# Rewriting a four-layer hedgehog and softmax attention block: token-major residual, visits of query to key chunks, projections between attention steps

## Chip, cores, metric

The kernel runs on one core of one Trainium2 chip. The metric is the device time of one execution in microseconds (us); lower is better. A single core has no second die to compare with, so runs are called fast when they lie within 1.5% of the fastest of the same kernel; all runs of changed kernels below are fast, except one single run whose state is unknown (e14_part1). Engines are named as in the profile: PE is TensorE (matmul), PEld its weight loads, DVE VectorE, ACT ScalarE, POOL GpSimd, SP SyncE, which here only issues DMAs (SPq).

## The reference, cut

```python
S, D, H = 2048, 1024, 32; Dh = 32                  # bf16 everywhere
def A(x, wqkv, w_phi, wo):                         # hedgehog linear attention
    q, k, v = heads(x @ wqkv)
    pq, pk = q @ w_phi, k @ w_phi                  # per head, 32 x 32
    phi_q = concat(softmax(pq), softmax(-pq)); phi_k = the same of pk
    kv, z = phi_k.T @ v, sum(phi_k)                # over all 2048 tokens
    return (phi_q @ kv) / (phi_q @ z + 1e-6) -> merge heads -> @ wo
def B(x, wqkv, wo):                                # plain softmax attention
    q, k, v = heads(x @ wqkv)
    return softmax(q @ k.T * Dh**-0.5) @ v -> merge heads -> @ wo
x = x + A(ln(x)); x = x + B(ln(x)); x = x + A(ln(x)); x = x + B(ln(x))
```

Every A layer needs a sum over all tokens (kv, z) before its query part can start. Every B layer has 32 x 2048 x 2048 exponentials.

## The kernel before

It runs one stage after the other. The residual is kept transposed (features on partitions). A B layer projects everything, then attends, then projects out:

```python
iters = [(g, qc, kc) for g in range(G) for qc in range(NQ) for kc in range(NT)]
...
for ii, (g, qc, kc) in enumerate(iters):
    ...
    for pr in range(2):                             # two heads each
        nc.scalar.activation(out=e[:], in_=s_cur[pr][:], func=ACT.Exp)   # 128 x 1024
    ...
    emit_scores(g2, qc2, kc2, s_next)               # 4 row-tiled matmuls, K = 32
    for j in range(4):                              # 4 column-tiled: values
        nc.tensor.matmul(out=num_ps[hsl, :], lhsT=v_aug[:, kc, g, ...], rhs=e_tiles[pr][...], ...)
    for j in range(4):                              # 4 column-tiled: denominators
        nc.tensor.matmul(out=den_ps[hsl, :], lhsT=ones_bf[:, 0:DH], rhs=e_tiles[pr][...], ...)
    if kc == NT - 1:
        nc.vector.reciprocal(out=rden[:], in_=den_ps[:])       # 128 x 512
        nc.vector.tensor_tensor(out=oT[:, g, q_sl], in0=num_ps[:], in1=rden[:], op=ALU.mult)
```

An A layer computes the key projection twice, once for exp(+pk) and once for exp(-pk) (`for b in range(2): ... emit_pk(fc, t)`), and layer norm sums over features with matmuls against ones.

The softmax here doesn't subtract the row's maximum and nothing guards it: scores larger than these inputs give would overflow.

## Time and profile before

3484.5 us (median of 2 runs; 3484.05 to 3484.96).

| stage | us | what is busy |
|---|---|---|
| A layer and B projections, first time | 0 to 750 | PE and DVE; ACT 242 us |
| attention | 750 to 1687.5 | ACT all the time |
| the same again | 1687.5 to 2440 | PE and DVE; ACT 244 us |
| attention | 2440 to 3377 | ACT all the time |
| last output projection, store | 3377 to 3483.5 | PE, then DVE |

The first lines of the page of the kernel before: busy time, share of the span and count by engine, then busy tenths in 40 slices, with the granted TensorE clock in tenths of full speed.

```profile
span 3483.5 us, 44252 instructions
PE 3190.9 (92%) x18316; PEld 1118.3 (32%) x18432; DVE 1359.2 (39%) x2009; ACT 2360.9 (68%) x2688; POOL 0.7 (0%) x6
...
PE   2898679999999999999979976899999999999998
...
ACT  0125861039999999999312298100999999999970
...
PEclk9999989999999999999999988999999999999997
```

PE at 92% suggests a PE-bound kernel, but PE busy time is no proof of that: the Trainium skill ("Trainium Kernel Development and Optimization", Performance Expectations) warns that matmul busy time is a bad measure of how near a kernel is to its limit, because matmuls are pipelined. This trace agrees: in attention PE counts as busy for 936 of 937.5 us, and yet the scores that it makes wait for ACT, as the lines below show. Two windows of the kernel before, columns being the stretch, its length, then busy time (count) of PE, PEld, DVE, ACT, POOL, granted clock, DMA share and GB/s:

```profile
750.00:1687.50 937.50, 936.35 (x6134) 271.05 (x6132) 125.53 (x62) 937.38 (x1023) 0.00 (x0) 1.00 0.00 1
2440.00:3377.00 937.00, 936.68 (x6132) 271.12 (x6132) 125.53 (x62) 937.00 (x1024) 0.00 (x0) 1.00 0.00 1
```

The timeline of ACT in the kernel before, at the start of attention and 150 us later (start, duration, what):

```profile
750.12 1.02 ACT L295 ACTIVATE E_5251<-sps_5243 128x1024 bf16<-128x1024 f32 x1 [70.11 <-PE sps_5244 L274]
751.05 1.02 ACT L295 ACTIVATE E_5253<-sps_5244 128x1024 bf16<-128x1024 f32 x1
...
900.19 1.29 ACT L295 ACTIVATE E_6752<-spsn_6738 128x1024 bf16<-128x1024 f32 x1
901.11 1.29 ACT L295 ACTIVATE E_6754<-spsn_6739 128x1024 bf16<-128x1024 f32 x1
```

One exponential starts every 0.915 us while each takes 1.02 us, later 1.29 us: each is already waiting in ACT when the one before is still running. ACT sets the pace of attention, 1024 x 0.915 = 937 us per layer. In the other 1610 us ACT is busy for 486 us. That is the room that the change aims at.

### The profile page before, as it was taken

To read this page: it belongs to the slowest core of one execution; us is meant where nothing else is said; L and a number is where in the kernel's file an instruction comes from. 1 tells how busy PE (TensorE), PEld (TensorE's weight loads), DVE (VectorE), ACT (ScalarE), POOL (GpSimd) and SP (SyncE) were. 2 spreads that over 40 slices of the span, in tenths; PEclk is the share of its full clock that TensorE was granted. 3 is DMA by queue.
4 is the path that set the end of the run, shared out by engine and by line. 5 is a ranking of instruction groups with operands and counts; after the bars stand their busy time and mean duration, and the time that the engine had idled before them with its cause. 6 is when DMAs were issued, how large, how long until landed. Compare 5 with 4: busy or idle time off the path is not lost.

```text
span 3483.5 us, 44252 instructions
## 1 busy us (share of the span) xinstructions
PE 3190.9 (92%) x18316; PEld 1118.3 (32%) x18432; DVE 1359.2 (39%) x2009; ACT 2360.9 (68%) x2688; POOL 0.7 (0%) x6
## 2 busy tenths in 40 slices
PE   2898679999999999999979976899999999999998
PEld 1343224432222222222334422344222222222223
DVE  2978876621111111111288888566011111111114
ACT  0125861039999999999312298100999999999970
POOL 0000000000000000000000000000000000000000
PEclk9999989999999999999999988999999999999997
DMA  6000001320000000000310000043000000000001
GB/s 132 15 1 1 1 25 61 128 78 1 1 1 1 1 1 1 1 1 1 74 49 1 1 1 0 25 145 121 1 1 1 1 1 1 1 1 1 1 25 49
DMA packets 112170, 82.67 MB, mean 24 GB/s; under 512 B 54624, under 2 KB 103776, under 8 KB 111968
## 3 DMA queue, kind: packets, MB, share of 16 engines
q1 hardware_dynamic: 111968, 79.84, 7.9%
q8 instruction: 144, 2.36, 0.3%
q14 instruction: 58, 0.48, 0.0%
HBM read 63.05 MB, written 4.19 MB: 19 GB/s over the span
## 4 chain that ended last, share of the span: by engine, by line
PE 75%; ACT 11%; DVE 10%; SPq 2%; issue 1%; DMA 1%; ACTq 0%; DVEq 0%
PE num_ps L307 19%; PE den_ps L319 13%; PE ps L167 7%; PE ps L222 6%; PE ps L245 3%; PE pkps L422 3%; ACT L548 2%; ACT L546 2%; DVE tmp L131 2%; ACT ebt L509 2%; DVE phik L449 1%; DVE xnT L134 1%; DVE ssum L445 1%; ACT e L441 1%; PE ps L142 1%
## 5 line engine op out<-in xcount | busy, mean ns | idle before, releaser
L330 DVE RECIPROCAL rden<-den_ps 128x512 f32<-128x512 f32 x64 | 214.9, 3358 | 1626.9 <-PE den_ps L319 1626.9
L274 PEld LDWEIGHTS <-kT 32*128 32x128 bf16 x4096 | 311.7, 91 | 872.8 <-issue 872.8
L307 PEld LDWEIGHTS <-v_aug 128*32 128x32 bf16 x4096 | 197.1, 93 | 465.6 <-issue 465.6
L222 PE MATMUL ps<-xnc,wslab 128*128 128x512 bf16 x1004 | 230.8, 386 | 15.2 <-DVE xnc L134 13.4
L167 PE MATMUL ps<-oT,wo_t 128*128 128x512 bf16 x1000 | 226.4, 386 | 16.2 <-DMA wo_t<-in_B_wo_dram 14.6
L422 PE MATMUL pkps<-W_pk,xnT 128*128 128x512 bf16 x994 | 239.2, 379 | 1.4
L441 ACT ACTIVATE e<-pkps 128x512 bf16<-128x512 f32 x128 | 76.2, 597 | 225.8 <-PE pkps L422 197.9
L117 ACT ACT_TABLE_LOAD x16 | 20.5, 1283 | 298.8 <-DVE t_386 L114 94.4
L319 PEld LDWEIGHTS <-ones_bf 128*32 128x32 bf16 x4096 | 208.8, 95 | 0.0
L491 PE MATMUL pqps<-xnT,W_pq 128*128 128x512 bf16 x496 | 160.7, 440 | 1.5 <-issue 0.7
L167 PEld LDWEIGHTS <-wo_t 128*128 128x128 bf16 x1024 | 101.7, 99 | 149.8 <-issue 33.9
L222 PEld LDWEIGHTS <-wslab 128*128 128x128 bf16 x1024 | 101.4, 99 | 142.8 <-issue 27.6
L142 PE MATMUL ps<-wv,xnT 128*128 128x512 bf16 x502 | 117.0, 380 | 21.6 <-DVE xnT L134 20.2
L174 DVE TENSOR_TENSOR xT<-xT,ps 128x512 bf16<-128x512 bf16 x128 | 87.4, 687 | 123.6 <-PE ps L167 121.7
L422 PEld LDWEIGHTS <-xnT 128*128 128x128 bf16 x1024 | 95.2, 98 | 91.6
L245 PE MATMUL ps<-wslab,xnc 128*128 128x512 bf16 x504 | 111.4, 379 | 0.4
L445 DVE TENSOR_REDUCE ssum<-e 128x16 f32<-128x512 bf16 x128 | 87.6, 685 | 39.6 <-ACT e L441 38.7
L449 DVE TENSOR_TENSOR phik<-e,rs 128x512 bf16<-128x512 bf16 x128 | 88.0, 691 | 11.8
L491 PEld LDWEIGHTS <-W_pq 128*128 128x128 bf16 x512 | 55.9, 110 | 92.0 <-issue 52.5
L546 ACT ACT_TABLE_LOAD x64 | 82.1, 1283 | 1.1
L548 ACT ACT_TABLE_LOAD x64 | 82.1, 1283 | 1.1
L509 ACT ACTIVATE ebt<-pqps 128x512 bf16<-128x512 f32 x128 | 74.5, 598 | 11.8 <-PE pqps L491 5.8
(9623 smaller groups left out, 7096.0 us busy)
## 6 DMA issues: line engine op xcount, KB each, us to landing
wslab<-in_B_wqkv_dram SPq DMA_DIRECT2D x48, 1024.0 KB, 5.0
wo_t<-in_A_wo_dram SPq DMA_DIRECT2D x2, 2048.0 KB, 9.7
wv<-in_A_wqkv_dram SPq DMA_DIRECT2D x2, 2048.0 KB, 7.9
wo_t<-in_B_wo_dram SPq DMA_DIRECT2D x2, 2048.0 KB, 8.8
out_dram<-tr SPq DMA_DIRECT2D x16, 256.0 KB, 2.0
phi<-in_A_w_phi_dram SPq DMA_DIRECT2D x64, 2.0 KB, 1.6
wqT<-in_A_wqkv_dram SPq DMA_TRANSPOSE x16, 4.2
wkT<-in_A_wqkv_dram SPq DMA_TRANSPOSE x16, 4.2
```

The source lines that it names most:

```text
L142: nc.tensor.matmul(ps[:], lhsT=xn_lhsT_fn(po), rhs=wv[:, po, fc * C512:(fc + 1) * C512], start=(po == 0), stop=(po == PO - 1),)
L167: nc.tensor.matmul(ps[:], lhsT=wo_t[:, po, ft * P:(ft + 1) * P], rhs=oT[:, po, cs], start=(po == 0), stop=(po == PO - 1),)
L222: nc.tensor.matmul(ps[:], lhsT=wt[:, po, gi * P:(gi + 1) * P], rhs=xnc[:, po, :], start=(po == 0), stop=(po == PO - 1),)
L245: nc.tensor.matmul(ps[:], lhsT=xnc[:, po, st * P:(st + 1) * P], rhs=wt[:, po, :], start=(po == 0), stop=(po == PO - 1),)
L274: nc.tensor.matmul(out=s_tiles[pr][:, jj * C512:(jj + 1) * C512], lhsT=kT[prt, g, k_sl], rhs=qT[prt, g, q_sl], start=True, stop=True, tile ...
L307: nc.tensor.matmul(out=num_ps[hsl, :], lhsT=v_aug[:, kc, g, j * DH:(j + 1) * DH], rhs=e_tiles[pr][:, jj * C512:(jj + 1) * C512], start=(kc ...
L319: nc.tensor.matmul(out=den_ps[hsl, :], lhsT=ones_bf[:, 0:DH], rhs=e_tiles[pr][:, jj * C512:(jj + 1) * C512], start=(kc == 0), stop=(kc == ...
L330: nc.vector.reciprocal(out=rden[:], in_=den_ps[:])
L422: nc.tensor.matmul(ps[:], lhsT=xnT[:, po, t * P:(t + 1) * P], rhs=W_pk[:, po, fc * C512:(fc + 1) * C512], start=(po == 0), stop=(po == PO ...
L491: nc.tensor.matmul(ps[:], lhsT=W_pq[:, po, g * P:(g + 1) * P], rhs=xnT[:, po, cs], start=(po == 0), stop=(po == PO - 1),)
L546: nc.scalar.activation(out=t3_list[gg][:], in_=t3_list[gg][:], func=ACT.Ln)
L548: nc.scalar.activation(out=t3_list[gg][:], in_=t3_list[gg][:], func=ACT.Exp, scale=-1.0)
```

## The change

The intent: keep ACT at its exponentials while PE does projections between them. The kernel becomes its own scheduler. A planner with a clock and estimated costs decides at build time in which order every engine gets its instructions. The core of it, cut (the diff replaces nearly every line):

```diff
+VISITS = (                        # (query chunk, key chunks, has parked sums, is last)
+    (0, (0,), False, False),      # visit 0
+    (1, (0, 1), False, False),    # visit 1
+    (0, (1,), True, False),       # visit 2
+    (2, (0, 1, 2), False, False), # visit 3
+    (0, (2, 3), True, True),      # visit 4
+    (1, (2, 3), True, True),      # visit 5
+    (2, (3,), True, True),        # visit 6
+    (3, (0, 1, 2, 3), False, True), # visit 7
+)
+    t_q, t_acc, t_part, t_R, t_tmp = tok(2), tok(3), tok(2), tok(2), tok(2)
...
+        for c in range(NC):       # chunks of 512 tokens
+            build_AQ(l, c)        # hedgehog query part
+            build_AO(l, c)        # its output projection, layer norm, transpose
+            build_BP(l + 1, c)    # QKV projection of the attention layer
+        for q in range(NC):
+            build_BO(l + 1, q)    # output projection of attention
+            if l == 0:
+                build_AK(2, q)    # hedgehog key part of the next A layer
...
+    def part_loader():            # load a parked sum from HBM, ahead of its unit
+        for u in units:
+            if u.part:
+                ...
+                b = yield from grab(t_part)
+                clk.start(part_load1(u, b))
+    def finish_unit(u):
+        if u.part:
+            yield ("key", ("pl", u))          # the parked sum has landed
+            yield tt("V", ..., a, a, acc_t[:], ALU.add)
+        acc_s.give(acc_t)                     # only now may the next unit sum
+        if not u.last:
+            yield dma(pd[k][:], a, 2.6)       # park it again
+            drop(token, b); return
+        R = yield from grab(t_R)
+        # reciprocal of 2 x 512 denominators, spread over 128 partitions by way of HBM
+        yield dma(dnd[i][:], a[d0:d0 + 64:32, :])
+        yield dma(rc[:], dnd[i][:].rearrange(...))
+        yield ("op", "V", 0.2, lambda e: nc.vector.reciprocal(out=rc[:], in_=rc[:]))
+        yield dma(rnd[i][:].rearrange(...), rc[:])
+        yield ("op", "D", ...)                # two DMAs that broadcast it
+        yield dma(r[n0 + 32:n0 + 64, :], ...)
+        yield tt("P", ..., otb[ko][...], a[...], r[...], ALU.mult)   # POOL
+        drop(t_R, R); drop(token, b)
```

A unit is one pair of heads in one visit. Its steps are four row-tiled score matmuls, two 128x1024 exponentials and eight column-tiled sum matmuls (row-tiled: each uses 32 rows of the PE array, column-tiled: 32 columns, so four stand side by side). A visit can start as soon as its key chunks are projected, which is why attention can begin after one chunk; the price is that a query chunk's sums have to be parked in HBM between its visits. Projections are issued between steps as groups of four column-tiled matmuls through the one PSUM bank ("bg") that attention leaves free. The second key projection of the A layers and the layer norm by matmul are gone; the residual is token-major, so the normalised rows go through DMA transposes.

## The prediction

> **What bounds the kernel now.** The busy-time table reads PE 92%, ACT 68%, DVE 39%, but by stage it splits in two. Attention runs from 750 to about 1687 and 2440 to about 3377 us (windows view): ACT is busy 750.0 of 750 us from 900 to 1650. The timeline shows one 128x1024 exponential starting every 0.915 us; it grows from 1.02 us (first) to 1.29 us (steady), so each queues behind the last: ACT saturated. 1024 x 0.915 = 937 us per layer, 1874 us in all. The other 1610 us are PE and DVE work with ACT mostly idle: 18 of 250 us busy from 500 to 750.
>
> **What the change does.** Exponentials of attention: the same 2048 of 128x1024. The floor of 1874 us stays. Removed: the second pass of pk projections (256 matmuls per A layer at 0.216 to 0.219 us, 110 us in all), the layer norm by matmul, 128 ACT table loads of 1.28 us, most 3.36 us reciprocals. Moved: projections go between attention steps as four-column-tile groups. The instruction order of the changed kernel shows 1934 such groups beside 2162 full matmuls.
>
> **Costing a step.** Trace: column-tile groups follow each other after 0.22 us; the switch from row-tiled scores (0.216) costs 0.32-0.216 = 0.10 us. A step owes 0.22 scores + 0.44 sums + about 0.2 switches = 0.86 us, leaving room for four background groups in 1.83 us. Issue rate should not bind: narrow matmuls with weight loads ran at 55 ns per pair, a group needs four pairs in 0.22. The Trainium skill ("TensorE: Matmul & The Clock Gate", part 3) says that small tiles run concurrently; the trace agrees (four row tiles of scores started within 10 ns at 749.65 us).
>
> **Sum**, counting from the instruction order the background between each pair of steps and taking max(1.833, 0.86 + background) per step:
> - before the first step: 191 us of PE work, DVE about as much; with load, transpose and layer-norm latency 255 us (estimate)
> - attention layer 1: 1097 us (three holes of 32 to 43 us of projections where a key chunk is not ready)
> - between the attention layers: 93 us of PE work plus serial latency: 135 us
> - attention layer 2: 1079 us
> - tail: last normalization, 64 matmuls, store: 25 us
> - not in these: hedgehog exponentials on ACT inside attention, about 50 us; DMA latency in the holes, 6 x 8; late scores and in-order stalls: a buffer's loop (0.47 + 1.02 + 0.06 + switch 0.1 + up to 0.22 waiting for a group) only just fits 1.83 us
>
> That gives about 2680 us.
>
> **What would show it.** ACT about 80% busy over the span, near 100% in long stretches; E activations 0.915 us apart, the first at about 255 us; a hole of about 135 us near the middle; column-tile groups at 0.22 us.
>
> **What would make it wrong.** Column-tiled groups costing clearly more than 0.22 us in a sustained stream (issue or weight loads): at 0.4 us both layers become PE-bound and the time passes 2900. A DMA issue held SP 0.37 to 0.42 us in the trace, a transpose 1.3 us; the kernel issues about 1700 in one in-order queue planned at 0.07 us, so waits at its head can hold up layer norm and Q loads. The static order can stall PE wherever real durations exceed the planned ones.
>
> Chances: faster 0.97, same 0.01, slower 0.02; 2680 us, 8 in 10: 2530 to 2880.

## The result

3045.0 us (median of 2; 3041.33 to 3048.71) against 3484.5 us. The ratio is 0.874 (95% interval 0.871 to 0.876). A ratio is the mean time of one kernel's fast runs over that of the other's of the same rounds, so not quite the ratio of the medians quoted. The change is faster by 12.6%, but 365 us slower than predicted, outside the range.

The first lines of the page of the changed kernel:

```profile
span 3046.9 us, 58388 instructions
PE 2480.4 (81%) x23978; PEld 871.6 (29%) x23978; DVE 981.5 (32%) x1812; ACT 2079.3 (68%) x2387; POOL 295.6 (10%) x330
...
PE   5887888879878877669888787987988888866888
...
ACT  2442649929929878359992172993995688846996
...
PEclk9998989689789689889968898976987977666767
```

ACT does as much as planned, but over 68% of the span and not 80%: its row has deep dents in the first half of each layer (slices down to 2) and mostly shallower ones in the second half (3 to 8). To size them, the 2048 exponentials were taken in order and cut into the eight visits of each layer (a visit has 64 exponentials per key chunk, so its floor is 58.6 us per key chunk at 0.915 us each). "Predicted" is the sum (1097 and 1079 us for the two layers), split afterwards by the same stretches by the recipe of the prediction, with PE's order in the trace; of the 90 us that it sets aside, 48 were for the holes as its text says, and the other 42 are put to the rest of attention.

| stretch | predicted, us | measured, us | difference |
|---|---|---|---|
| before the first exponential | 255 | 277 | +22 |
| six holes without exponentials, before visits 1, 3, 4 of each layer | 219, and 48 allowed | 377 | +110 |
| visits 4, 5, 6, both layers (floor 586) | 632 | 830 | +198 |
| the other visits, both layers | 1325, and 42 allowed for ACT work and stalls | 1403 | +36 |
| between the attention layers | 135 | 137 | +2 |
| after the last exponential | 25 | 24 | -1 |

So two stretches hold most of the miss. The windows of the changed kernel for them, a hole (355 to 424) and a visit 6 (2656 to 2779), and visit 7 after it for comparison:

```profile
355.20:424.20 69.00, 48.04 (x297) 23.07 (x300) 35.50 (x73) 6.58 (x14) 13.65 (x20) 0.83 0.54 151
...
2656.00:2778.80 122.80, 72.42 (x588) 20.05 (x581) 18.67 (x38) 60.60 (x66) 17.65 (x14) 0.61 0.29 84
2778.80:3023.30 244.50, 212.60 (x1800) 51.67 (x1800) 24.72 (x44) 235.50 (x257) 22.77 (x18) 0.72 0.11 29
```

In the hole ACT is busy 6.6 of 69 us and PE 48. In visit 6 no engine is busy: ACT 60.6 of 122.8 us, PE 72, DVE 19. Nothing that is counted by busy time bounds visit 6; something that is held must. The chain in visit 6 of the second layer, from three timelines of the changed kernel (SP's DMA issues, then DVE, then POOL; the two `blk<-pd` are the loads of two parked sums, `dn`, `rc`, `rn` are the hops of the reciprocal):

```profile
2701.82 0.84 SPq L309 DMA_DIRECT2D blk<-pd  x2
2705.22 0.50 SPq L309 DMA_DIRECT2D dn<-blk  x1
2706.85 0.32 SPq L309 DMA_DIRECT2D rc<-dn  x1
...
2710.97 0.32 SPq L911 DMA_DIRECT2D Q<-qd  x1
2711.38 0.50 SPq L912 DMA_DIRECT2D Q<-qd  x1
2711.93 0.58 SPq L309 DMA_DIRECT2D Q<-qd  x1
2712.60 0.54 SPq L309 DMA_DIRECT2D rn<-rc  x1
...
2717.89 0.84 SPq L309 DMA_DIRECT2D blk<-pd  x2
```

```profile
2704.50 0.69 DVE L327 TENSOR_TENSOR blk<-blk,acc 128x512 f32<-128x512 f32 x1 [4.08 <-DMA blk<-pd]
...
2708.60 0.20 DVE L963 RECIPROCAL rc<-rc 128x8 f32<-128x8 f32 x1 [0.73 <-DMA rc<-dn]
```

```profile
2716.95 1.25 POOL L327 TENSOR_TENSOR oTB<-blk,blk 64x512 bf16<-64x512 f32 x1 [12.17 <-DMA blk<-rn]
```

Two parked sums are loaded together at 2701.8 us, and the next two at 2717.9 us. In between each goes through load, addition, four DMA hops, a 0.20 us reciprocal and a POOL multiply. That is two units per 16.1 us, 8.05 us per unit, where two steps of exponentials need 3.7. The planner has two tokens for parked sums (`t_part = tok(2)`), and one is given back only after the POOL multiply. Over the 96 units of visits 4 to 6 the medians are 4.5 us from issue of the load to end of the addition and 12.8 us from there to the end of the multiply, 17.1 us in all; two tokens make 8.6 us per unit of it, and visits 4 to 6 took 830 / 96 = 8.65. (The 16.6 and 8.3 us of the expectations below leave out most of the multiply itself.) That the two agree says only that both tokens were nearly always taken. What held the units up is in the wait before the addition. The same line of the pages with one token (e14_part1), with two (the changed kernel) and with six (e1_tokens):

```profile
L327 DVE TENSOR_TENSOR blk<-blk,acc 128x512 f32<-128x512 f32 x128 | 87.8, 686 | 644.4 <-DMA blk<-pd 628.5
L327 DVE TENSOR_TENSOR blk<-blk,acc 128x512 f32<-128x512 f32 x128 | 87.8, 686 | 279.1 <-DMA blk<-pd 146.0
L327 DVE TENSOR_TENSOR blk<-blk,acc 128x512 f32<-128x512 f32 x128 | 87.3, 682 | 186.8 <-PE acc L1150 171.5
```

With one token nearly all, with two about half of DVE's wait before the addition ended with the load of the parked sum, which came late; with six the load came early and DVE waited for PE's sums. One more thing is in the lines of SP: the reciprocal ended at 2708.8 us, but its result was sent only at 2712.6, behind three Q loads that the plan had put before it.

The hole in the changed kernel, by PE's timeline:

```profile
380.70 0.95 PE L762 MATMUL ring<-kvm,blk 128*128 128x128 bf16 x7
384.97 3.59 PE L344 MATMUL bg<-slab,blk 128*128 128x512 bf16 x8 [3.31 <-DMA blk<-blk]
388.35 3.02 PE L344 MATMUL ring<-slab,blk 128*128 128x512 bf16 x8
391.21 1.89 PE L344 MATMUL bg<-slab,blk 128*128 128x512 bf16 x8
...
399.84 1.89 PE L344 MATMUL ring<-slab,blk 128*128 128x512 bf16 x8
409.90 1.01 PE L344 MATMUL bg<-xnT,slab 128*128 128x512 bf16 x2 [8.17 <-DMA xnT<-blk]
```

PE runs the query part of the hedgehog, waits 3.3 us for a DMA transpose, runs its output projection, waits 8.2 us for layer norm and the next transpose, and then starts the QKV projection that attention waits for. When each of these two waits ends, the records show a clock of 0.5, for 3 to 6 us more in each of the six holes: eight matmuls of 512 columns take 3.59 us, then 1.89. Counting matmul starts 0.22 us apart as work, PE stood still for 22 to 27 us of each of the six holes. The prediction had allowed 8.

And PE's clock is lower in the second half of the second layer: 0.71 in visits 4 to 7, against 0.84 in those of the first layer and 0.85 to 0.86 in the first halves. The timeline of PE of the changed kernel in a stretch where ACT is 100% busy, and which has no projections:

```profile
2956.80 0.61 PE L1146 MATMUL acc<-E,V 128*32 128x512 bf16 x2
2956.81 0.61 PE L1150 MATMUL acc<-E,ones 128*32 128x512 bf16 x2
...
2958.41 0.39 PE L1146 MATMUL acc<-E,V 128*32 128x512 bf16 x2
2958.42 0.39 PE L1150 MATMUL acc<-E,ones 128*32 128x512 bf16 x2
2958.64 0.38 PE L1146 MATMUL acc<-E,V 128*32 128x512 bf16 x2
```

Four column tiles start together, and groups follow each other after 0.23 us at full clock (2958.41 to 2958.64): the packing works as predicted. But 1.6 us earlier the same matmuls take 0.61 us. The records show a granted clock of 1.0 and 0.5 in turn, 0.68 on average from 2900 to 3000 us. This was not in the prediction, and it gives a rival explanation. (A first doubt: visits 4 to 6 took 435 us in the first layer at 0.82 to 0.88, and 395 us in the second at 0.61 to 0.79.)

### The profile page after: what moved, and what is told of

It is laid out like the page before. It is cut to its first block, busy times and chain, and to the rows that moved or that the text cites. A ratio compares the mean times of both kernels' runs of the same rounds, so it can differ in the third digit from the quotient of the medians.

```text
span 3046.9 us, 58388 instructions
## 1 busy us (share of the span) xinstructions
PE 2480.4 (81%) x23978; PEld 871.6 (29%) x23978; DVE 981.5 (32%) x1812; ACT 2079.3 (68%) x2387; POOL 295.6 (10%) x330
## 5 line engine op out<-in xcount | busy, mean ns | idle before, releaser
L1098 ACT ACTIVATE E<-ring 128x1024 bf16<-128x1024 f32 x2048 | 1910.7, 1084 | 668.2 <-PE ring L1115 486.9
L1146 PE MATMUL acc<-E,V 128*32 128x512 bf16 x4096 | 775.4, 468 | 116.4 <-DVE blk L327 113.0
L1150 PE MATMUL acc<-E,ones 128*32 128x512 bf16 x4096 | 775.1, 468 | 0.0
L1115 PE MATMUL ring<-Q,K2b 32*128 32x512 bf16 x2048 | 472.8, 452 | 136.3 <-ACT E L1098 122.9
L1115 PE MATMUL ring<-Q,K2a 32*128 32x512 bf16 x2048 | 469.6, 455 | 15.7 <-ACT E L1098 11.4
L341 PE MATMUL bg<-xnT,slab 128*32 128x512 bf16 x4120 | 281.3, 387 | 26.1 <-DVE K2b L322 12.7
L1146 PEld LDWEIGHTS <-V 128*32 128x32 bf16 x4096 | 163.6, 102 | 465.5 <-issue 446.6
L327 POOL TENSOR_TENSOR oTB<-blk,blk 64x512 bf16<-64x512 f32 x124 | 159.8, 1289 | 1104.4 <-DMA blk<-rn 1042.0
L341 PE MATMUL bg<-slab,xnT 128*32 128x512 bf16 x2220 | 159.2, 409 | 21.2 <-ACT blk L605 8.3
L1150 PEld LDWEIGHTS <-ones 128*32 128x32 bf16 x4096 | 154.6, 101 | 3.9
```

Source lines behind the costliest of these rows:

```text
L327: return ("op", e, cost, lambda x: eng(x).tensor_tensor(out=o, in0=a, in1=b, op=op))
L341: nc.tensor.matmul(o[js], lhsT=l[:, js], rhs=r, start=st, stop=sp, tile_position=(0, 32 * j), skip_group_check=True)
L1098: yield ("op", "S", c_act(1024), lambda x: nc.scalar.activation(out=E[:], in_=ring_t[buf][:], func=ACT.Exp, scale=INV_SQRT_DH))
L1115: nc.tensor.matmul(ring_t[bufs[e]][:, j, :], lhsT=K2[e][c][r, u.g, m, :], rhs=u.Q[r, e, :], start=True, stop=True, tile_position=(r0, 0), ...
L1146: nc.tensor.matmul(u.acc[n0 + 32 * j:n0 + 32 * j + 32, :], lhsT=Vc[c][:, kt, DH * h:DH * (h + 1)], rhs=E[:, j, :], start=first, stop=final ...
L1150: nc.tensor.matmul(u.acc[d0 + 32 * j:d0 + 32 * j + 32, :], lhsT=ones[:], rhs=E[:, j, :], start=first, stop=final, tile_position=(0, d0 + 3 ...
```

## The experiments

Theories at the start. **T**: two tokens for parked sums limit visits 4 to 6. **C**: PE at half clock limits them. **S**: waits at the head of SP's one queue, planned at 0.07 us per issue where a DMA issue holds SP 0.41 us (median of 1618) and a transpose 1.25 us (median of 96). Later **L**: the holes are a serial chain that nothing is planned beside. And **O**: a last one about output tiles. All results were correct. Times are medians, with the lowest and highest of the runs in brackets; ratios are to the kernel before, in the same rounds. The runs came in three series on three chips; the kernel before had a median of 3486 to 3487 us in each, so runs of different series can be compared to about 0.1%. The record labels e1_tokens, e2_fast, e3_fill and e5_tok_fill "unclear": in their series two of seven executions of the kernel before were slow (3693 and 3694 us, clock 0.90). The ratios leave these out, and their 95% intervals lie below the change's 0.871 to 0.876, that of e3_fill (0.867 to 0.870) only just.

A slip in the expectations: "693 us" for visits 4 to 6 was added up wrongly; it is 830 us, with an excess of 244 us over the floor, as the same text also says. e1_tokens raised the reciprocal tiles as well, but they were not a second limit of the changed kernel: by its code a unit of visits 4 to 6 takes one only while it holds a token, so two tokens never need more than two tiles.

### e1_tokens: more parked sums in flight

```diff
-    t_q, t_acc, t_part, t_R, t_tmp = tok(2), tok(3), tok(2), tok(2), tok(2)
+    t_q, t_acc, t_part, t_R, t_tmp = tok(2), tok(3), tok(6), tok(5), tok(2)
```

> Edit: the planner may have 6 parked sums (was 2) and 5 reciprocal tiles (was 2) in flight. Theory T (the finish of a parked unit holds one of two tokens for 16.6 us, so units cannot follow each other faster than 8.3 us, against 3.7 or 7.3 us of exponentials): visits 4 to 6 of both layers, which took 693 us against 586 us of exponentials (holes and small gaps 244 us with the stage edges), lose most of that: total 2820 to 2900 us. Rival C (PE at half clock in these stages is what slows them): no change, 3045 +- 25. Rival S (waits at the head of the one DMA queue): little change, 3000 to 3060.

Measured: 2920.8 us (2920.0 to 2935.6), ratio 0.839; 124 us less than the change. Visits 4 to 6 fell from 830 to 699 us (second layer's visit 6 from 123 to 77), while the start and the holes stayed within 5 us each, and the first layer's visit 7 grew by 16. That refutes C as the main cause and bears T out, but the gain is 21 us short of the range: the first layer's visits 5 and 6 kept 73 us of excess (see e12_bo).

### e2_fast: shorter hold, same tokens

```diff
                 units.append(Unit(l, vi, q, ks, p, part, last))
+                units[-1].fast = part and last
```

> Edit: two tokens as before, but units of visits 4 to 6 take the 3.36 us reciprocal on DVE in place of four DMA hops, so a token is held about 9.5 us instead of 16.6. Theory T: at least 4.75 us per unit, visit 6 falls from 147 and 123 us to about 80 each, visits 4 and 5 go to their floors: total 2830 to 2920 us. Rival C: no change. Rival S: faster too, because some 500 DMAs leave the queue; then the first holes shrink as well.

Measured: 2919.7 us (2913.6 to 2928.2), ratio 0.838. The way from the addition to the end of the multiply fell from 12.8 to 4.9 us (medians of visits 4 to 6). Shortening it does as much as adding tokens, which is what T says of a limit of the form tokens / time held. The total is at the upper edge of what was expected; visit 6 missed: 134 and 95 us instead of about 80, and no run took that apart. The first hole (67.9 us) did not shrink, but that says nothing of S, though the expectation thought so: the 480 DMAs that left the queue (96 units, five each) all belong to visits 4 to 6, which come after the holes of their layer. What speaks against S in the holes is e6_tok_issue below.

### e3_fill: keep the clock up

```diff
+            if att_active() and bg_free[0] and clk.heap[0][0] - st["t"] >= MM and "phibd" in clk.keys:
+                set_mode("col")
+                emm(bg_t[:], phibd[:, 0, :], phibd[:, 0:4, :].rearrange("p g n -> p (g n)"), True, True, True)
+                st["t"] += MM
+                continue
             st["t"] = max(st["t"], clk.heap[0][0])
```

> Edit: 1068 groups of four useless matmuls go into the background bank where the plan has PE idle inside attention, so that PE stays busy and its clock is granted. Theory T: granted clock rises well over 0.83, time changes little (3000 to 3060 us). Rival C: visits 4 to 7 lose their excess, 2850 us or less.

Measured: 3028.6 us (3024.9 to 3030.3), ratio 0.869: 16 us less. The windows of visits 4 to 7 of the second layer, first of the changed kernel, then of this one:

```profile
2383.90:3023.30 639.40, 515.86 (x4724) 137.61 (x4717) 91.81 (x183) 534.62 (x576) 78.40 (x62) 0.71 0.23 66
```

```profile
2373.80:3004.40 630.60, 572.80 (x7802) 205.39 (x7795) 91.14 (x183) 532.64 (x576) 78.64 (x62) 0.98 0.23 67
```

The granted clock went from 0.71 to 0.98, and the stretch became 9 us shorter. C is out for visits 4 to 7: the half clock is real, but lifting it gained 16 us in all. The fill does not act in the holes, where the clock stayed as it was (0.83 in the first).

### e5_tok_fill: both

> Edit: both the tokens and the filler matmuls. Theory T: within 30 us of the tokens alone. If after the tokens are there PE at half clock becomes the next limit, 40 us or more below the tokens alone.

Measured: 2931.7 us (2921.9 to 2937.2), ratio 0.840; not better than the tokens alone. The clock is not the next limit either.

### e6_tok_issue: true issue costs in the plan

```diff
-        return ("op", "D", 0.07, lambda e: nc.sync.dma_start(out=o, in_=i), lat)
+        return ("op", "D", 0.4, lambda e: nc.sync.dma_start(out=o, in_=i), lat - 0.33)
-        return ("op", "D", 0.07, lambda e: nc.sync.dma_start_transpose(out=o, in_=i), 4.6)
+        return ("op", "D", 1.25, lambda e: nc.sync.dma_start_transpose(out=o, in_=i), 3.42)
```

The same 0.07 is replaced in the three places that issue a DMA directly. Only the order of instructions can change by this.

> Edit: the tokens of e1_tokens, and the plan charges a DMA issue 0.40 us and a transpose 1.25 us of the queue, as the trace shows, instead of 0.07. Theory S (planned order does not fit the queue, waits at its head delay chains): 30 us or more below the tokens alone (2921). Theory T plus serial holes: within 25 us of it.

Measured: 2883.0 us (2879.8 to 2889.1), ratio 0.827; 38 us below the tokens alone. So S is true as well, at a tenth of the miss. The six holes changed by 2 us each at most, so S is not what made them. It was run on top of the tokens only; with two tokens, waits in the queue are part of the time that a token is held, as the 3.8 us before `rn<-rc` above.

### e9_order: the next chunk's query part before this chunk's QKV

```diff
-        for c in range(NC):
-            build_AQ(l, c)
-            build_AO(l, c)
-            build_BP(l + 1, c)
+        build_AQ(l, 0)
+        for c in range(NC):
+            build_AO(l, c)
+            if c + 1 < NC:
+                build_AQ(l, c + 1)
+            build_BP(l + 1, c)
```

The slots for normalised activations are handed out in the same new order, and a counter test `== 4` became `% 10 == 4`: as it stood, it never released a token when one of four tasks ended before the last had started, which stopped the planner. So this edit is two edits. Rebuilding the plans without a chip showed that the counter also fails once in the changed kernel itself: from the third chunk of the first A layer on, its planner has four of its six tokens for hedgehog exponentials, and 20 of 22 buffers. The planner's own clock, which is a plan and no run, ends at 2841 us for the changed kernel, at 2723 with the counter mended alone, and at 2599 with the new order too.

> Edit: the tokens of e1_tokens, and the query part of hedgehog chunk c+1 is listed before the QKV projection of chunk c instead of after it (a counter that would leak a token then is mended). Theory L (each of the holes of 57 to 69 us before visits 1, 3 and 4 is 38 us of projections and 24 us of PE waiting for a serial chain): start 15 to 22 us later, the hole before visit 4 gone, that before visit 3 about half, that before visit 1 shorter by some 10 us; total 2720 to 2800 us. Rival V (holes are PE work that has to be done somewhere, order only moves it): 2890 to 2940 us.

Measured (with the tokens): 2715.2 us (2711.9 to 2716.7), ratio 0.778; 206 us below the tokens alone, beyond the expected range. The holes before visits 1, 3, 4 went from 68, 58, 62 us to 45, 14, 0 in the first layer, and from 66, 64, 60 to 45, 14, 0 in the second; the start came 15 us later and the time between the layers grew by 20. V, that the work only moves, is refuted. L's waiting is gone, but how much of that is the order's doing and how much the mended counter's was not run; in the plan the mend alone shortens the holes before visits 3 and 4 and leaves those before visit 1 as they were.

### e16_order_only: the order and the mended counter without the tokens

> Edit: the changed kernel with the new order of chunks alone, two tokens as before. Theories T and L are about different stages, so the gains add: 206 us below the changed kernel, 2820 to 2860 us, visits 4 to 6 still at 800 us or more. If they overlap: above 2890 us.

Measured: 2819.9 us (2817.0 to 2827.4), ratio 0.809; 225 us below the change, at the lower edge of what was expected, while visits 4 to 6 stayed at 819 us. The two windows of the holes that are left in the first layer:

```profile
374.20:418.90 44.70, 39.48 (x295) 20.10 (x296) 27.61 (x59) 11.11 (x23) 12.98 (x19) 1.00 0.62 187
608.60:623.00 14.40, 13.30 (x72) 6.19 (x73) 7.05 (x11) 0.82 (x4) 3.03 (x5) 1.00 0.89 216
```

The first hole has as many PE instructions as the 69 us hole of the changed kernel (295 and 297), but PE is now busy 39 of 45 us at full clock, before 48 of 69 at 0.83. What went is waiting, and the half clock that follows it. The gains of order and tokens add up to within 20 us: 225 + 124 = 349 alone, 330 together.

### e14_part1: one parked sum in flight

```diff
-    t_q, t_acc, t_part, t_R, t_tmp = tok(2), tok(3), tok(2), tok(2), tok(2)
+    t_q, t_acc, t_part, t_R, t_tmp = tok(2), tok(3), tok(1), tok(2), tok(2)
```

> Edit: the changed kernel with one parked sum in flight instead of two, a dose control. Theory T: one unit per 16.6 us in visits 4 to 6, 265 us per visit, 1590 us for the six against 830 measured with two: total about 3750 us (3600 to 3850). If it was the reciprocal tiles or anything else that limited: below 3300 us.

Measured: 3449.6 us (one run, state unknown). Much slower, as T says and the other reading excludes, but outside the range, since a token was not held as long as with two: with one unit at a time the medians are 3.6 us to the end of the addition and 8.9 us to the end of the multiply, 12.5 in all. Visits 4 to 6 took 1199 us, 12.5 us for each of their 96 units. With two tokens it is 830 us, 8.65 per unit, against 17.1 / 2 = 8.6. Tokens / time held gives the rate in both; I had taken the time held for a constant. The window of visit 6, second layer:

```profile
2997.50:3174.90 177.40, 80.03 (x514) 21.30 (x509) 18.59 (x38) 60.36 (x66) 18.89 (x15) 0.58 0.20 59
```

ACT has its 60 us of work in 177 us.

### e10_order_issue, e11_order_fast: on top of e9_order

> Edit: e9_order and the true issue costs in the plan. Theory S: 30 us or more below e9_order. Otherwise within 25 us.

Measured: 2679.0 us (2675.7 to 2682.0), ratio 0.768; 36 us below e9_order, nearly the 38 us of e6_tok_issue. S again.

> Edit: e9_order, and visit 6 alone takes the 3.36 us reciprocals on DVE. Theory T: visit 6 was 109 and 77 us with the tokens; DVE needs about 4.75 us per unit, 76 us per visit, so the first layer's visit 6 gains 20 to 30 us and the second's nothing; total 15 to 35 us below e9_order.

Measured: 2712.7 us (2709.9 to 2714.7), ratio 0.778; the same as e9_order, a miss. Visit 6 took 111 and 87 us, no better than 109 and 79. Once there are tokens enough, the length of the reciprocal is not what holds visit 6 up. That left the question of what does.

### e12_bo, e13_bo_otb: output tiles

In e10_order_issue the first layer still had a hole of 26 us in visit 6 and one of 20 us in visit 7, the second layer had one of 10 us only (end to start; the expectation counts from start to start). The first layer's background has key tasks of the next A layer, listed ahead of the output projections that give the output tiles back.

```diff
             build_BO(l + 1, q)
-            if l == 0:
-                build_AK(2, q)
+            if l == 0 and q:
+                build_AK(2, q - 1)
+        if l == 0:
+            build_AK(2, NC - 1)
```

and, for e13_bo_otb, one more line:

```diff
-    otb_s = Slots(clk, [sb(f"oTB{i}", [P, C]) for i in range(9)])
+    otb_s = Slots(clk, [sb(f"oTB{i}", [P, C]) for i in range(11)])
```

> Edit: e10_order_issue with the output projection of query chunk q+1 listed before the key part of the next layer's chunk q. Theory O (what is left in visits 6 and 7 of the first layer, holes of 27 and 21 us, is units waiting for one of 9 output tiles, which 8 output-projection tasks give back late because they queue behind key tasks for the one background bank): those holes shrink, total 2630 to 2665 us. Otherwise within 15 us of 2679.

Measured: 2652.6 us (2649.9 to 2654.7), ratio 0.761 against 0.768; 26 us below e10_order_issue. The first layer's visits 6 and 7 fell from 104 and 274 us to 89 and 262, so the order was a cause, as O says.

> Edit: e12_bo and 11 output tiles instead of 9. Theory O: 5 to 25 us below e12_bo; otherwise equal to it.

Measured: 2643.9 us (2636.9 to 2646.8), ratio 0.758 (0.756 to 0.760) beside 0.761 (0.759 to 0.762): the intervals overlap, so these 9 us are not settled, though visit 6 went to 81 and 64 us (from 89 and 72), and its longest hole from 15 and 11 us to 7 and under 5, as O says. It is the fastest version found: 24% below the kernel before and 13% below the change. Its page and its window between the attention layers:

```profile
span 2645.1 us, 60959 instructions
PE 2310.1 (87%) x25233; PEld 841.5 (32%) x25292; DVE 973.8 (37%) x1793; ACT 2084.9 (79%) x2406; POOL 294.2 (11%) x330
...
ACT  2442456997999999789993345599799999999996
```

```profile
1405.60:1557.90 152.30, 122.02 (x756) 59.81 (x772) 98.14 (x184) 32.20 (x60) 27.43 (x40) 0.91 0.49 141
```

Visits 4 to 6 now take 636 us, which is what the prediction had summed for them (632). What is left of ACT's idle time is the 298 us at the start and the 152 us in the middle, where the sum over all tokens forbids an earlier start.

## Why the prediction was wrong

**Right.** ACT saturation and the floor: wherever they are not held up, exponentials start 0.904 us apart (median over the changed kernel), a little faster than the 0.915 us that was assumed. The packing: the prediction took from the Trainium skill ("TensorE: Matmul & The Clock Gate", part 3) that small tiles run concurrently, and the changed kernel's trace agrees: groups of four follow each other after 0.216 us (median of all neighbouring groups; 0.427 where the clock is halved), so the issue rate of PE did not bind. The hole between the attention layers (137 us for 135), the tail (24 for 25) and the direction were right.

**Wrong, first: "taking max(1.833, 0.86 + background) per step".** This counts engines and forgets the end of a unit. A unit with parked sums holds one of two tokens for 17.1 us, 0.9 us of it addition and reciprocal on DVE, 1.3 us the multiply on POOL, and the rest DMA latency, queueing and the wait for its own sums; units cannot follow each other faster than half of that. Visits 4 to 6 took 830 us for 632 summed. The plan's own limits (`tok(2)`) stood in the code that I read; I costed the reciprocal chain as work removed from DVE and not as latency added to a unit. e1_tokens, e2_fast and e14_part1 show it from three sides.

**Wrong, second: "DMA latency in the holes, 6 x 8".** The mechanism was named, the size was not: PE stood still 22 to 27 us in each, and the six took 377 us where 219 + 48 were summed. I had counted the matmuls before a hole's end and one latency; the trace has a chain of two transposes, DVE and POOL work in turn, and the half clock at the end of each wait. e9_order and e16_order_only show that it was waiting, since nearly the same work with other work beside it lost 206 and 225 us; that their edits also gave back leaked tokens leaves open why the planner had put nothing beside it.

**What both steps left out was in the plan.** The recipe took the order of PE's instructions from the planner, but not the planner's clock. That clock has 732 us for visits 4 to 6 and 359 us for the six holes, and ends at 2841 us: 161 of the 365 us were there before any run.

**Named and smaller.** The prediction listed waits at the head of SP's queue as a risk. They cost 36 to 38 us (e6_tok_issue, e10_order_issue, both on top of the tokens).

**Not foreseen and nearly harmless.** The half clock of PE during attention. It would have been an easy story, as the clock and the time went wrong together; e3_fill shows that it is not the cause.

**Open.** The start was 22 us longer than predicted, and no run took that apart. Edits of tokens also change the planned order, so a gain of one includes what the planner made of it; that the wait before the addition follows the tokens from one to two to six is the best evidence that this part is small. The order of chunks and the mended counter were not run apart; in the plan the mend is 118 of the 242 us that e16_order_only gains. What the half clock costs in the holes was not run by itself.

## What to carry to other kernels

When a profile stretch has no busy engine, look for what is held and for how long: the rate is holders divided by the time held, and DMA round trips belong to that time even if they cost no engine anything. A sum of engine times per step is a lower bound only; before believing it, walk once through the longest dependent chain of a unit and through every pool with two slots. If a planner with a clock made the order, read that clock first. Fill a serial chain with the next chunk's independent work by listing it earlier, and check a suspicious clock by keeping the engine busy before blaming it.

## What the Trainium skill lacked or had wrong

- "TensorE: Matmul & The Clock Gate", Why this matters for your kernels, advises no PE-idle gaps over about 3 us to avoid throughput drops. Taken alone that row misleads: here the clock fell to 0.68 on average (2900 to 3000 us of the changed kernel) although the longest stretch with no matmul in flight, by the records, was 0.53 us. The same page's section on a second failure mode does say that frequent micro-idles between groups of matmuls make the clock oscillate. What it lacks is how little work is too little. One pair of numbers: the kernel before held 1.00 with as many attention matmuls (658 recorded in 100 us, here 656), but they started in 329 groups (starts over 50 ns apart), here in 212. At the 0.216 us from group to group that is about 71 against 46 us of work in 100 (an estimate). Useless matmuls between them brought the clock back to 0.98 (e3_fill).
- The same table's advice to keep TensorE busy is about matmul throughput, and it lacks when that is worth nothing: raising the clock from 0.71 to 0.98 over visits 4 to 7 of the second layer gained 9 of 639 us, since PE was not the limit.
- "DMA: Bandwidth & Descriptors", Anatomy of one DMA, gives a fixed cost of about 2.0 us per DMA, for DMAs issued from GpSimd; for a whole DMA issued from SP it has no such figure. The hops here, issued from SP, come near it with one unit in flight: the four hops, a 0.20 us reciprocal and the POOL multiply took 8.9 us together in e14_part1. With two units in flight, 12.8 us.
- The same page (Issuing engines are not separate DMA queues) says that spreading DMAs over engines saves only issue time, which is usually small, and gives about 50 ns for dispatch on GpSimd's path; it has no figure for SP. On SP the records show 0.41 us per DMA issue (median of 1618) and 1.25 us per transpose (median of 96), 841 us of the 3047 in all, and a plan that knew it was 36 to 38 us faster.
